# Layer 2's down product in seven block products, with a planned order of instructions

## The chip, the cores and the metric

One core of a Trainium2 chip runs the whole program. The metric is device time in microseconds (us), the median of several runs. The engines that the text speaks of are PE (TensorE, matmuls; PEld is its weight load), ACT (ScalarE), DVE (VectorE), POOL (GpSimd) and SP (SyncE, which issues most of the DMA transfers). Each runs its own instructions in a fixed order and waits on semaphores for the others.

## The reference

A long convolution by FFT, and then two feed-forward layers on the 6016 tokens that come out of it, all in fp32:

```python
X = np.fft.rfft(x, axis=1)                      # x: (2, 3008, 256)
y = np.fft.irfft(X * (filt_r + 1j * filt_i), n=3008, axis=1)
x = y.reshape(6016, 256)
...
h = x @ w_in                                    # layer 1: (256, 2048), (2048, 256)
g = np.where(h >= 1, h, np.where(h <= -1, 0.0, (h + 1) ** 2 / 4))
x = g @ w_out
...
h = x @ w_in2                                   # layer 2, the same sizes
g = h / (1 + np.exp(-h))
return g @ w_out2
```

## The kernel before

**Numbers as sums of two.** Each fp32 factor of a product in the two layers is held as a high part (rounded to the fp32r format by ACT) and a low part (the remainder, a subtraction on DVE, or on POOL for weights). A product is then three matmuls: high by high, high by low, low by high. A matmul here is 128x128 weights by 128x502 (or 128x500) columns.

**The tiling.** The 2048 hidden units are 16 strips of 128, taken as 8 pairs j. The tokens are 12 blocks of about 501, taken as 6 pairs p. The first half of layer 1 (pairs 0 to 2, up to 368.6 us) is worked block by block, while the FFT of the second batch and the preparation of the weights run beside it. From there on comes a list of nine token pairs (`PL`): layer 1's last three, then all six of layer 2. For each of the nine pairs and each j there is one step (`group`), 72 steps in all. A step forms the 2x2 blocks of h (two strips by two token blocks, over two halves of the 256 inputs) by Strassen's scheme in its Winograd form: seven block products (`prod`) in place of eight, 21 matmuls, in three PSUM banks b, c and d. `snap` copies a state of b to SBUF (s1, u2, u4), and DVE adds these to d or c to form the blocks 11, 22 and 21; block 12 is b's last state. Each block then goes through its activation (`Chain.first`, `square`, `last`), is split into high (`high`, ACT, L592) and low (`low`, DVE, L595), and goes down: `down2` multiplies it by the two strips of w_out, 6 matmuls for each of the four blocks, 24 a step, accumulated over j in the banks a0, a1, b0, b1. The down product of step q-1 is issued in the four gaps of step q (`between`). So a step has 45 matmuls on PE.

**What sets the order.** The order in which the code calls the engines is the order of each queue: `group` is written out by hand, and an agenda (`at`, `due`) puts the preparation of operands and weights into numbered slots, four to a step (slot `GA + 4 * q` is the start of step q). Token operands of a pair are seven sums or blocks, split on ACT and DVE during the pair before (`split_x2`, L538; `rest_x2`, L543; `sum_x`, L533). For layer 1, `load_block` forms x by the FFT's last stage, fp32 matmuls (L333). Layer 2's weights are summed, rounded and split once (`sum_weight`, `round_weight`, `rest_weight`: DVE, ACT, POOL) around the start of layer 2, and then lie in SBUF to the end. Outputs are stored from ACT's queue and from SP's (`evict`).

```python
        accumulate(acc[p, n], W[m, j][mate], (chain.gh, chain.gl), first, last)
...
                down2(prev[("11", "22", "12", "21")[i]], (0, 1, 1, 0)[i], (0, 1, 0, 1)[i])
            due(GA + 4 * q + i)
```

## Time and profile before

| | |
|---|---|
| runs | 1140.82, 1142.73 and 1149.37 us, median 1142.73 us |
| span of the profiled execution | 1142.1 us |
| FFT and first half of layer 1 | 0 to 368.6 us |
| second half of layer 1, 24 Strassen steps | 368.6 to 638.0 us |
| layer 2, 48 Strassen steps | 638.0 to 1132.6 us |
| the rest, with the last stores | 1132.6 to 1142.1 us |
| busy share of the span | PE 98%, ACT 73%, DVE 67%, POOL 22% |

The span runs from the first to the last instruction of one execution, and lies 0.6 us under the median of the runs. Matmuls are pipelined, and each row of one is longer (0.39 us) than the distance to the next; how fast PE goes is read from the number of matmuls in a stretch.

### The profile page before, as it was taken

What the parts mean: (1) busy time and instruction counts of PE and PEld (TensorE: products, weight loads), DVE (VectorE), ACT (ScalarE), POOL (GpSimd) and SP (SyncE); (2) the same over time, 40 slices, a digit from 0 to 9 for tenths busy, and PEclk for the clock granted to TensorE, in tenths of its full rate; (3) what the DMA queues carried; (4) which work ended last, traced back from release to release, by engine and by line L of the source; (5) the groups of instructions that cost most, each with busy time, mean ns of one, the idle gap of its engine ahead of it and who ended that gap; (6) DMA issues with size and microseconds to landing.
All of it is one profiled execution on the core that took longest, in us unless ns stands there. A gap on an engine that the chain in (4) does not pass through costs nothing.

```text
span 1142.1 us, 14102 instructions
## 1 busy us (share of the span) xinstructions
PE 1116.0 (98%) x4931; PEld 902.2 (79%) x4931; DVE 764.4 (67%) x1212; ACT 830.2 (73%) x1532; POOL 250.4 (22%) x220
## 2 busy tenths in 40 slices
PE   9899999999999999999999999999999999999998
PEld 3477787787887787888887778888888888888887
DVE  7977656878769788767777766555555555455543
ACT  6788777878767688878888876766666666666654
POOL 5777535657523111000012141000000000000000
PEclk9899999999999999999999999999999999999999
DMA  9433032444221000100211220200200200200100
GB/s 206 130 102 100 3 118 83 136 118 135 92 96 61 28 1 1 37 1 1 81 38 28 76 71 1 72 1 1 73 1 1 73 1 1 73 1 1 37 1 36
DMA packets 34231, 60.33 MB, mean 53 GB/s; under 512 B 3792, under 2 KB 18352, under 8 KB 34160
## 3 DMA queue, kind: packets, MB, share of 16 engines
q1 hardware_dynamic: 30448, 53.03, 15.6%
q10 hardware_dynamic: 3712, 6.40, 1.6%
q8 instruction: 38, 0.62, 0.3%
q14 instruction: 33, 0.27, 0.1%
HBM read 42.90 MB, written 16.52 MB: 52 GB/s over the span
## 4 chain that ended last, share of the span: by engine, by line
PE 76%; DVE 10%; ACT 6%; issue 4%; POOL 2%; DMA 2%; SPq 0%; ACTq 0%; DVEq 0%; POOLq 0%
PE o L395 13%; PE o L394 13%; PE o L396 13%; PE b L547 5%; PE b L549 5%; PE b L548 5%; PE c L547 3%; PE xp L333 3%; PE c L549 3%; PE c L548 3%; PE h L361 2%; DVE we L179 2%; PE h L363 2%; PE h L362 2%; DVE gl L382 2%
## 5 line engine op out<-in xcount | busy, mean ns | idle before, releaser
L394 PE MATMUL o<-gh,wh 128*128 128x502 f32 (+1 forms) x624 | 244.5, 392 | 1.0 <-DVE ob L406 0.7
L395 PE MATMUL o<-gl,wh 128*128 128x502 f32 (+1 forms) x624 | 244.2, 391 | 0.9 <-DVE gl L595 0.6
L396 PE MATMUL o<-gh,wl 128*128 128x502 f32 (+1 forms) x624 | 243.6, 390 | 0.0
L595 DVE TENSOR_TENSOR gl<-c,gh 128x502 fp32r<-128x502 f32 (+1 forms) x288 | 191.2, 691 | 39.9 <-ACT gh L592 39.7
L592 ACT ACTIVATE gh<-c 128x502 fp32r<-128x502 f32 (+1 forms) x288 | 168.1, 617 | 5.7 <-DVE c L584 2.8
L556 ACT ACTIVATE u<-b 128x502 f32<-128x502 f32 (+1 forms) x144 | 83.9, 583 | 106.0 <-PE b L549 105.8
L394 PEld LDWEIGHTS o<-gh,wh 128*128 128x128 f32 x624 | 117.6, 188 | 27.0 <-DVE ob L406 1.5
L395 PEld LDWEIGHTS o<-gl,wh 128*128 128x128 f32 x624 | 117.7, 189 | 26.8 <-DVE gl L595 2.8
L396 PEld LDWEIGHTS o<-gh,wl 128*128 128x128 f32 x624 | 117.6, 188 | 24.5
L669 DVE TENSOR_TENSOR c<-c,u 128x502 f32<-128x502 f32 (+1 forms) x72 | 48.9, 679 | 97.9 <-ACT u L556 97.9
L571 ACT ACTIVATE c<-c 128x502 f32<-128x502 f32 (+1 forms) x144 | 88.7, 616 | 26.9 <-DVE c L669 25.4
L380 ACT ACTIVATE gh<-g 128x502 fp32r<-128x502 f32 (+1 forms) x96 | 59.8, 623 | 54.6 <-PE o L396 30.5
L382 DVE TENSOR_TENSOR gl<-g,gh 128x502 fp32r<-128x502 f32 (+1 forms) x80 | 64.3, 804 | 47.3 <-ACT gh L380 47.2
L688 DVE TENSOR_TENSOR c<-c,u 128x502 f32<-128x502 f32 (+1 forms) x72 | 48.9, 679 | 64.1 <-PE c L549 63.9
L556 ACT ACTIVATE s<-b 128x502 f32<-128x502 f32 (+1 forms) x72 | 42.5, 590 | 61.1 <-PE b L549 59.9
L361 PE MATMUL h<-xh,wh 128*128 128x502 f32 (+1 forms) x192 | 76.8, 400 | 3.6 <-DVE g L374 3.6
L374 DVE SCALAR_TENSOR_TENSOR g<-u,h 128x502 f32<-128x502 f32 (+1 forms) x96 | 64.3, 670 | 23.3 <-ACT u L373 23.3
L363 PE MATMUL h<-xh,wl 128*128 128x502 f32 (+1 forms) x192 | 75.1, 391 | 1.3 <-POOL wl L198 1.3
L362 PE MATMUL h<-xl,wh 128*128 128x502 f32 (+1 forms) x192 | 74.7, 389 | 0.0
L632 DVE TENSOR_TENSOR c<-d,s 128x502 f32<-128x502 f32 (+1 forms) x72 | 48.8, 678 | 37.0 <-ACT s L556 33.4
L367 ACT ACTIVATE u<-h 128x502 f32<-128x502 f32 (+1 forms) x96 | 55.4, 577 | 13.9 <-PE h L363 13.4
L584 DVE SCALAR_TENSOR_TENSOR c<-v,c 128x502 f32<-128x502 f32 (+1 forms) x72 | 49.2, 689 | 22.4 <-ACT v L579 22.1
(199 smaller groups left out, 2414.0 us busy)
## 6 DMA issues: line engine op xcount, KB each, us to landing
f<-in_filt_dram SPq DMA_DIRECT2D x47, 192.0 KB, 3.4
raw<-in_moe_w_in_dram SPq DMA_DIRECT2D x32, 256.0 KB, 2.7
raw<-in_moe_w_out_dram SPq DMA_DIRECT2D x32, 256.0 KB, 3.1
w2d<-wa SPq DMA_DIRECT2D x16, 256.0 KB, 3.4
wb<-w2d SPq DMA_DIRECT2D x16, 256.0 KB, 2.8
xs<-x2d SPq DMA_DIRECT2D x8, 502.0 KB, 4.6
Z<-in_x_dram SPq DMA_DIRECT2D x16, 192.0 KB, 4.9
x<-in_x_dram SPq DMA_DIRECT2D x16, 192.0 KB, 3.6
```

Of the source, the lines that this page charges most:

```text
L361: nc.tensor.matmul(h, wh[:, s], xh[:, k, :t], start=(k == 0), stop=False)
L362: nc.tensor.matmul(h, wh[:, s], xl[:, k, :t], start=False, stop=False)
L363: nc.tensor.matmul(h, wl[:, s], xh[:, k, :t], start=False, stop=(k == 1))
L394: nc.tensor.matmul(o[e], wh[:, s], gh, start=first, stop=False)
L395: nc.tensor.matmul(o[e], wh[:, s], gl, start=False, stop=False)
L396: nc.tensor.matmul(o[e], wl[:, s], gh, start=False, stop=last)
L547: nc.tensor.matmul(bank, wh, xh, start=first, stop=False, skip_group_check=True)
L548: nc.tensor.matmul(bank, wh, xl, start=False, stop=False, skip_group_check=True)
L549: nc.tensor.matmul(bank, wl, xh, start=False, stop=True, skip_group_check=True)
L556: nc.scalar.activation(v, src, AF.Copy)
L592: nc.scalar.activation(self.gh, self.g, AF.Copy)
L595: nc.vector.tensor_tensor(self.gl, self.g, self.gh.bitcast(F32), ALU.subtract)
```

## The change

Nothing changes in what is computed. Up to the end of layer 1's first half two orders change: the down product of a slot stands ahead of the splits of that slot and of the FFT's last stage, and so do its evictions. From the Strassen part on:

- **Down in seven products.** In layer 2 four steps (four j) make a unit group h, 12 of them. The four blocks of each step give four differences or sums on DVE (`combine`: T3, T2, T4, T1), seven operands are split (`halves`), and 7 products by blocks and sums of w_out, for each of 4 j, are 28 units of three matmuls (`UNITS`, `unit`), in place of 96 matmuls. They accumulate in three banks and a fourth (`D`) that takes a copy; `post` adds the results to the outputs, over two unit groups for each token pair. A step has seven gaps, with a unit in each; in layer 2's first four steps there are fewer, and what is left over stands at the end.
- **Snapshots from bank to bank.** The first product of a step is issued in the step before (`start`), ACT copies bank b to bank d, and the second product accumulates upon it, in place of a copy to SBUF and an addition on DVE. The two other snapshots go to SBUF as before.
- **Weights of layer 2.** In steps 11 to 21 the blocks and sums of layer 2's weights are formed, split and stored to memory (`stage2`, `sums2`, `round2`, `rest2`, `store2`). The up weights are then loaded again for each of the 48 steps into a ring of four (`load_up`, 896 KB each); the down weights are loaded once over layer 1's (`load_down`).
- **A planned order.** From `nc.hold()` on, every call is queued, and a planner with a time for each kind of instruction gives them out: PE in the order of the code, each other engine by the earliest start and then by what PE needs first. All stores go through SP. [...]

```diff
-    nc = tc.nc
+    nc = Planner(tc.nc)
...
+        if engine == "PE":
+            busy = n / 2400 + 0.019 if "32r" in ins[0][5] else n / 600 + (0.067 if n < 128 else 0)
+            return busy, busy + 0.19, False
+        if engine == "ACT":
+            busy = n / 1400 + (0.11 if psum else 0.152)
+            return busy, busy + 0.15, False
+        if engine == "DVE":
+            busy = n / 960 + 0.065
+            return busy, busy + 0.14, len(ins) - psum >= 2
+        busy = n / 425 + 0.06
+        return busy, busy + 0.17, True
...
+                for op in q[:1] if e == "PE" else q:
+                    if op.left:
+                        continue
+                    ready = max([o.done for o in op.need if e != "PE" or o.engine != e], default=0.0)
+                    start = max(ready, free)
+                    if op.port:
+                        start = max(start, self.ports["POOL" if e == "DVE" else "DVE"])
+                    key = (start, op.due, op.at)
...
+    def rest2(j, i):
+        h, q = (flat2(j, hl, i // 2)[:, i % 2 * 448:(i % 2 + 1) * 448] for hl in (1, 0))
+        nc.gpsimd.tensor_tensor(q.bitcast(F32R), q, h, ALU.subtract)
...
+    def load_up(g):
+        nc.sync.dma_start(upr[g % 4].bitcast(F32), w2u[g % NP])
...
+    DOWN = {1: ("A11", "a", "B"), 2: ("A12", "c", "D"), 6: ("S2", "a", "B"), 7: ("S3", "b", "C"),
+            5: ("S1", "a", "B"), 3: ("S4", "d", "B"), 4: ("A22", "c", "C")}
...
+        def start(self):
+            self.prod(self.b, "A11", "B11", True)
+            nc.scalar.activation(self.d, self.b, AF.Copy)
...
+        def halves(self, name):
+            h, l = rot("gh")[:, :self.n], rot("gl")[:, :self.n]
+            nc.scalar.activation(h, self.v(name), AF.Copy)
+            nc.vector.tensor_tensor(l, self.v(name), h.bitcast(F32), ALU.subtract)
+            return h, l
+
+        def combine(self):
+
+            for name, to, x0, x1, op_, need in (
+                ("T3", "b", "d", "b", ALU.subtract, {"T3"}), ("T2", "a", "a", "b", ALU.add, {"T3", 1}),
+                ("T4", "c", "c", "a", ALU.subtract, {"T2", 2}), ("T1", "a", "d", "a", ALU.subtract, {"T4", 6}),
+            ):
...
+        k.prod(k.d, "A12", "B21", False)
+        gap(0)
+        k.act("a", k.d)
+        k.prod(k.b, "S2", "T2", False)
+        k.snap("c")
+        gap(1)
...
+    EXTRA = {1: (2, 3), 2: (2, 3), 3: (2, 6)}
+    AHEAD, LOOK = 3, 1
```

The three places on which the prediction rests most, as the built programs have them.

The start of the Strassen part, PE before: bank b0, bank d0, then the leftover down product of layer 1's first half (o, from gh and gl).

```order
L396 MATMUL o5_1_3460<-gh5_10_3647,wl0_10_995 128x500
L547 MATMUL b0_0_3774<-xr_3349,wh0_0_483 128x502
L548 MATMUL b0_0_3774<-xr_3349,wh0_0_483 128x502
L549 MATMUL b0_0_3774<-xr_3349,wl0_0_484 128x502
L547 MATMUL d0_0_3780<-xr_3349,wh0_0_483 128x502
L548 MATMUL d0_0_3780<-xr_3349,wh0_0_483 128x502
L549 MATMUL d0_0_3780<-xr_3349,wl0_0_484 128x502
L394 MATMUL o5_0_3459<-gh5_11_3675,wh0_11_1053 128x500
```

PE now: h_2 is the bank d, h_0 the bank b, and o_b0 the bank of the down product.

```order
L152 MATMUL o_b1_94<-gh_3_83,wl0_11_1051 128x500
L156 MATMUL h_2_3600<-wh0_0_518 128x512
L156 MATMUL h_0_3598<-xr_3200,wh0_0_518 128x502 x2
L156 MATMUL h_0_3598<-xr_3200,wl0_0_519 128x502
L156 MATMUL h_2_3600<-xr_3200,wh0_0_518 128x502 x2
L156 MATMUL h_2_3600<-xr_3200,wl0_0_519 128x502
L156 MATMUL o_b0_93<-gh_0_80,wh0_12_1105 128x500
```

ACT at that place, before and then now; gh is the rounding of the last block of the first half.

```order
L380 ACTIVATE gh5_14_3757<-g5_14_3729 128x500
L373 ACTIVATE u5_15_3755<-u5_15_3755 128x500
L380 ACTIVATE gh5_15_3770<-g5_15_3754 128x500
L556 ACTIVATE s10_0_3778<-b0_0_3774 128x502
L556 ACTIVATE u20_0_3809<-b0_0_3774 128x502
```

```order
L152 ACTIVATE gh_2_82<-g5_14_3553 128x500
L152 ACTIVATE u5_15_3577<-u5_15_3577 128x500
L152 ACTIVATE gh_3_83<-g5_15_3576 128x500
L156 ACTIVATE h_2_3600<-h_0_3598 128x502
L156 ACTIVATE wh0_5_720<-sl_wa2_3614 128x128
```

One row of the leftover down product has gone ahead, and bank d, which waits for ACT's copy of b, now stands ahead of the others; the copy has the place of the snapshot s1, behind the rounding of the last block.

DVE in the middle of layer 2, before: one step and the next one's first rows.

```order
L632 TENSOR_TENSOR c115_3_8064<-d5_3_8060,s15_3_8058 128x500
L595 TENSOR_TENSOR gl21_5_2_8068<-c215_2_8038,gh21_5_2_8067 128x500
L595 TENSOR_TENSOR gl11_5_3_8083<-c115_3_8064,gh11_5_3_8082 128x500
L543 TENSOR_TENSOR xr_3349<-xs6_0_7884,xr_3349 128x502
L669 TENSOR_TENSOR c225_3_8104<-c5_3_8095,u45_3_8102 128x500
L688 TENSOR_TENSOR c215_3_8122<-c5_3_8095,u25_3_8086 128x500
L595 TENSOR_TENSOR gl22_5_3_8125<-c225_3_8104,gh22_5_3_8124 128x500
L595 TENSOR_TENSOR gl12_5_3_8128<-c125_3_8117,gh12_5_3_8127 128x500
L543 TENSOR_TENSOR xr_3349<-xs6_1_7886,xr_3349 128x502
L632 TENSOR_TENSOR c115_4_8149<-d5_4_8145,s15_4_8143 128x500
```

DVE now, some two thirds of a step: sl_ and ob are buffers of blocks, h_3 the bank c.

```order
L156 TENSOR_TENSOR sl_raw_3611<-sl_raw_3611,sl_g10_5833 128x500
L156 TENSOR_TENSOR gl_0_84<-sl_raw_3611,gh_0_80 128x500
L156 TENSOR_TENSOR xr_3200<-xs_1_3226,xr_3200 128x502
L156 TENSOR_TENSOR gl_1_85<-sl_g1_5824,gh_1_81 128x500
L156 TENSOR_TENSOR sl_wa0_3612<-h_3_3601,sl_wa0_3612 128x500
L156 TENSOR_TENSOR gl_2_86<-sl_g6_5829,gh_2_82 128x500
L156 TENSOR_TENSOR sl_raw_3611<-sl_raw_3611,sl_g6_5829 128x500
L156 TENSOR_TENSOR xr0_3616<-xs_1_3226,xr0_3616 128x502
L156 TENSOR_TENSOR gl_3_87<-sl_g0_5823,gh_3_83 128x500
L156 TENSOR_TENSOR sl_g1_3607<-sl_wa0_3612,sl_g1_3607 128x500
L156 TENSOR_TENSOR sl_g2_5825<-h_3_3601,sl_g2_5825 128x500
```

Seven remainders (gl) a step in place of four, two additions from a bank in place of three, and the differences between SBUF blocks are new.

DVE at the end of the program, before and then now.

```order
L595 TENSOR_TENSOR gl11_8_7_10463<-c118_7_10445,gh11_8_7_10462 128x500
L669 TENSOR_TENSOR c228_7_10483<-c8_7_10474,u48_7_10481 128x500
L688 TENSOR_TENSOR c218_7_10500<-c8_7_10474,u28_7_10466 128x500
L595 TENSOR_TENSOR gl22_8_7_10503<-c228_7_10483,gh22_8_7_10502 128x500
L595 TENSOR_TENSOR gl12_8_7_10506<-c128_7_10495,gh12_8_7_10505 128x500
L595 TENSOR_TENSOR gl21_8_7_10518<-c218_7_10500,gh21_8_7_10517 128x500
L406 COPY ob1_11p_1_10542<-o2_8_1_1_9981 128x500
L406 COPY ob1_10p_1_10554<-o2_8_0_1_9964 128x500
```

```order
L156 TENSOR_TENSOR gl_2_86<-sl_raw_3611,gh_2_82 128x500
L156 TENSOR_TENSOR gl_3_87<-sl_g3_5826,gh_3_83 128x500
L156 TENSOR_TENSOR sl_raw21_5839<-o_b0_93,sl_raw21_5839 128x500
L156 TENSOR_TENSOR gl_0_84<-sl_we_3610,gh_0_80 128x500
L156 TENSOR_TENSOR gl_1_85<-sl_wa0_3612,gh_1_81 128x500
L156 TENSOR_TENSOR gl_2_86<-sl_g1_3607,gh_2_82 128x500
L156 TENSOR_TENSOR gl_3_87<-ob_1_89,gh_3_83 128x500
L156 TENSOR_TENSOR sl_wl1_5841<-o_b1_94,sl_wl1_5841 128x500
L156 TENSOR_TENSOR sl_raw21_5839<-o_a1_92,sl_raw21_5839 128x500
L156 TENSOR_TENSOR sl_wh1_5840<-o_b0_93,sl_wh1_5840 128x500
```

Where the last step's two additions, four remainders and two copies stood, a run of splits, differences and additions into the outputs (sl_raw, sl_wl, sl_wh from banks o) now ends the program; of DVE, 37 instructions come after the last up product, of PE 69 matmuls.

## Rows read from the trace of the kernel before

**Rows 1.** The page, part 1: busy us, share, instructions

```profile
PE 1116.0 (98%) x4931; PEld 902.2 (79%) x4931; DVE 764.4 (67%) x1212; ACT 830.2 (73%) x1532; POOL 250.4 (22%) x220
```

**Rows 2.** Stretches of the Strassen part, with clock and DMA

```profile
core 0: us, PE busy (x) PEld busy (x) DVE busy (x) ACT busy (x) POOL busy (x), PEclk, DMA share, GB/s
...
368.57:384.61 16.04, 12.07 (x52) 9.46 (x51) 13.09 (x23) 10.96 (x23) 3.10 (x3) 1.00 0.05 17
384.61:400.61 16.00, 16.00 (x98) 14.22 (x97) 10.73 (x21) 10.35 (x20) 1.69 (x2) 1.00 0.09 33
400.61:637.97 237.36, 234.14 (x1041) 191.05 (x1040) 185.20 (x315) 199.35 (x374) 19.00 (x17) 1.00 0.07 23
...
648.22:661.36 13.14, 11.05 (x47) 8.25 (x45) 8.50 (x13) 9.74 (x19) 6.71 (x6) 1.00 0.67 208
661.36:1122.39 461.03, 461.03 (x2027) 381.72 (x2025) 248.55 (x393) 302.91 (x549) 11.04 (x9) 1.00 0.07 23
```

**Rows 3.** Waits of PE, PEld, 368 to 662 us: total, times, longest

```profile
PE c L547 <- DVE c L669: 3.6, 5, 1.7
...
PEld c L547 <- DVE c L669: 6.6, 7, 2.1
```

**Rows 4.** Timeline, PE, the last matmul of the kernel

```profile
1137.81 0.38 PE L396 MATMUL o<-gh,wl 128*128 128x500 f32 x1
```

**Rows 5.** Timeline of the first step: start, us, instruction, idle before

```profile
371.78 0.49 PE L547 MATMUL d<-xr,wh 128*128 128x502 f32 x1 [2.36 <-DVE g L374]
...
375.09 0.67 DVE L374 SCALAR_TENSOR_TENSOR g<-u,h 128x500 f32<-128x500 f32 x1
...
375.85 0.62 ACT L380 ACTIVATE gh<-g 128x500 fp32r<-128x500 f32 x1 [0.88 <-DVE g L374]
376.38 0.57 ACT L556 ACTIVATE s<-b 128x502 f32<-128x502 f32 x1
...
377.05 0.47 PE L547 MATMUL b<-xr,sh 128*128 128x502 f32 x1 [1.61 <-issue]
```

**Rows 6.** Timeline of ACT in layer 2, a PSUM source and then SBUF sources

```profile
803.35 0.59 ACT L571 ACTIVATE c<-b 128x502 f32<-128x502 f32 x1
803.84 1.13 ACT L592 ACTIVATE gh<-c 128x502 fp32r<-128x502 f32 x2
```

**Rows 7.** Timeline of DVE, 427 to 432 us

```profile
427.33 0.67 DVE L533 TENSOR_TENSOR xs<-xs 128x502 f32<-128x502 f32 x1
427.92 1.27 DVE L584 SCALAR_TENSOR_TENSOR c<-v,c 128x502 f32<-128x502 f32 x2
429.11 0.68 DVE L533 TENSOR_TENSOR t<-xs,xs 128x502 f32<-128x502 f32 x1
429.70 0.68 DVE L669 TENSOR_TENSOR c<-c,u 128x502 f32<-128x502 f32 x1
430.29 2.09 DVE L595 TENSOR_TENSOR gl<-c,gh 128x502 fp32r<-128x502 f32 x2
```

**Rows 8.** Groups of POOL, 400 to 700 us: busy us, mean ns, idle before

```profile
L452 POOL TENSOR_TENSOR wl<-wb,wh 128x512 fp32r<-128x512 f32 x10 | 13.2, 1340 | 46.3 <-ACT wh L449 46.3
L452 POOL TENSOR_TENSOR sl<-ws,sh 128x384 fp32r<-128x384 f32 x8 | 9.7, 1218 | 23.0 <-ACT sh L449 23.0
```

**Rows 9.** DMA issues: KB each, median us to landing

```profile
xs<-x2d SPq DMA_DIRECT2D x8, 502.0 KB, 4.6
...
wb<-w2d SPq DMA_DIRECT2D x16, 256.0 KB, 2.8
```

**Rows 10.** The remainders of the down operands on DVE, layer 2

```profile
L595 DVE TENSOR_TENSOR gl<-c,gh 128x502 fp32r<-128x502 f32 (+1 forms) x180 | 120.0, 687 | 37.0 <-ACT gh L592 37.0
```

**Rows 11.** Timeline of POOL beside rows 7

```profile
430.34 1.50 POOL L452 TENSOR_TENSOR s<-ws,s 128x384 fp32r<-128x384 f32 x1 [9.00 <-ACT s L449]
```

**Rows 12.** A stretch in which the granted clock fell

```profile
40.00:45.80 5.80, 3.88 (x11) 1.65 (x10) 5.76 (x10) 4.18 (x7) 4.72 (x5) 1.00 0.00 2
45.80:52.60 6.80, 5.95 (x18) 3.74 (x17) 5.32 (x10) 3.32 (x6) 5.08 (x5) 0.50 0.24 80
```

More of the change, by code (lines that the diff above doesn't have):

```diff
@@ L494, in up_weight, with up_part, down_part @@
+    def up_part(g, which):
+        a = ORDER.index(which) * 128
+        return [upr[g % 4][:, i, a:a + 128] for i in range(2)]
+    def down_part(j, which):
+        t, c = divmod(7 * j + ORDER.index(which), 4)
+        return [dw[t, i][:, c * 128:(c + 1) * 128] for i in range(2)]
     def up_weight(m, j, which):
@@ new lines, in second_slots, with third_slots @@
+    def second_slots():
+        free[:] = [t for t in free if t.tensor.name not in retired]
+        for t in fixed["wa"]:
+            spare(t)
+    def third_slots():
+        for i in range(13):
+            spare(gp.tile([128, PMAX], F32, name=f"sl_g{i}"))
+        for i in range(2):
+            spare(rings["ob"][i])
+            spare(rawp.tile([128, 1024], F32, tag="raw2", name=f"sl_raw2{i}", bufs=2), 2)
+            for v in "hl":
+                spare(pools["w"].tile([128, 512], F32, tag=f"w{v}", name=f"sl_w{v}{i}"))
+        for name in ("11", "21", "22", "12"):
+            fixed[name] = free.pop()
@@ new lines, in mark_written, with post @@
+    def mark_written(bank):
+        w = weights[0, 0][0]
+        nc.tensor.matmul(bank, w[:, :128], w, start=True, stop=True, skip_group_check=True)
+    def post(h, r, n):
+        i, jj = UNITS[r]
+        if jj != CH - 1:
+            return
+        pair, half = divmod(h, 2)
+        name = {1: "11", 2: "11", 6: "21", 5: "22", 7: "22", 3: "12", 4: "21"}[i]
+        v, src = fixed[name][:, :n], down_bank(h, DOWN[i][2])[:, :n]
+        if i == 1:
+            nc.scalar.activation(down_bank(h, "D")[:, :n], src, AF.Copy)
+        elif i in (2, 6, 5, 3) and half == 0:
+            nc.scalar.activation(v, src, AF.Copy)
+        else:
+            nc.vector.tensor_tensor(v, src, v, ALU.add)
+        if half == 1 and i in (2, 7, 3, 4):
+            e, k = int(name[0]) - 1, int(name[1]) - 1
+            t0 = BLOCKS[2 * pair + k][0]
+            nc.sync.dma_start(out[e * 128:(e + 1) * 128, t0:t0 + n], v)
@@ new lines, in unit, with step, gap @@
+    def unit():
+        u = count["unit"]
+        count["unit"] += 1
+        pump(u)
+        h, r, i, q = unit_of(u)
+        a, _, to = DOWN[i]
+        n = groups[q].n
+        first = UNITS[r] in ((1, 0), (7, 0))
+        triple(down_bank(h, to)[:, :n], down_part(groups[q].j, a), parts.pop(u), first)
+        post(h, r, n)
+        pump(u + AHEAD)
+    def step(q, done=range(7)):
+        k = groups[q]
+        prev = groups.get(q - 1)
+        halves = [("a", 0), ("a", 1), ("d", 0), ("d", 1), ("b", 0), ("b", 1), ("c", 0), ("c", 1)]
+        def gap(i):
+            if i % 2 == 0:
+                spare_bank[0] = k.other
+                due(GA + 4 * q + i // 2)
+            if q <= Q2:
+                if prev:
+                    for name, e in halves[i:i + 1 if i < 6 else i + 2]:
+                        prev.down(name, e)
+                else:
+                    for fn in left.get(i, ()):
+                        fn()
+            elif q >= Q2 + CH or i in EXTRA[q - Q2]:
+                unit()
+        if prev:
+            prev.act("c")
+            prev.cut_up("c")
+        k.prod(k.d, "A12", "B21", False)
[4 more added lines that the diff above has]
+        gap(1)
+        k.cut_up("a")
+        k.prod(k.c, "S3", "T3", True)
+        gap(2)
+        k.prod(k.b, "S1", "T1", False)
+        k.snap("d")
+        k.join("d")
+        gap(3)
+        if q + 1 < STEPS:
+            groups[q + 1] = Group(q + 1)
+            groups[q + 1].start()
+        k.act("d")
+        k.cut_up("d")
+        gap(4)
+        k.prod(k.b, "S4", "B22", False)
+        k.act("b", k.b)
+        if k.m:
+            k.combine()
+        gap(5)
+        k.cut_up("b")
+        k.prod(k.c, "A22", "T4", False)
+        k.join("c")
+        gap(6)
+        if k.m and q + 4 < STEPS:
+            load_up(q + 4)
+        marks[q + 1] = nc.mark()
@@ L864, in tile_fft_conv_moe_moe @@
             rest = up(c, f)
+            if i >= LAG:
+                down(*slots[i - LAG])
             if len(gq) > 1:
```

577 lines of the change are left out of this document (355 added, 222 removed).

## Prediction

> **What bounds the kernel now.** I read the shares of busy time first, then the Strassen part by stages, then the waits inside the stages. PE is busy for 98% of the span, DVE for 67% and ACT for 73% [rows 1]. In layer 2 this is no average over gaps: between 661.36 and 1122.39 us PE is busy for all of 461.03 us, at full clock, with 2025 weight loads, one for each matmul [rows 2]. That is 0.2277 us for a matmul and 10.25 us for a step of 45. DVE is busy for 54% of this stretch and ACT for 66%. So layer 2 gets faster with fewer matmuls, until DVE or ACT is full.
>
> In the second half of layer 1 there is a little besides matmuls. The first step has 51 matmuls (its 21 and the 30 of five leftover down products), 11.6 us, and takes 16.04 [rows 2]: 4.4 us of waiting. The second takes 16.00, 5.75 over 10.25, which are the FFT's last stage for the next pair (PE is busy throughout). Steps 2 to 23 take 237.36; less 22 x 10.25 and once more 5.75, 6.1 us of waiting, mostly for DVE's additions that free bank c [rows 3]. The second step of layer 2 takes 13.14, 2.9 too many [rows 2]. After the last matmul at 1137.81 + 0.23 [rows 4] the span runs on for 4.1 us, with the last copy and store. In all some 13 us of the Strassen part are waits; the rest is the number of matmuls.
>
> **The change, part by part.**
>
> *Matmuls.* Each of 12 unit groups has 28 x 3 = 84 in place of 4 x 24 = 96, so 144 fewer, and two markers more: 142 x 0.2277 = 32.3 us less of PE. This is certain in number, since the built orders show it.
>
> *The first step.* In the trace ACT rounds the last block of the first half at 375.85, because DVE forms it only at 375.09, and takes the snapshot behind it at 376.38; PE goes on at 377.05 [rows 5]. DVE's backlog there belongs to the part that isn't planned, and its order is kept. The copy from bank to bank has the snapshot's place in ACT's order, but now bank d waits for it, and the leftover down products stand behind d. So by 377.05 PE has done 10 matmuls since 368.57 (six that were moved ahead, a marker, three for b) where it did 18 before. From 377.05 on, 3118 matmuls are left (3122 of the Strassen part less four): 709.9 us. With two last stages of 5.75, PE alone ends at 1098.5, and with the 4.1 us behind it the span is 1102.6. To that come waits.
>
> The copy itself, PSUM to PSUM on ACT, stands nowhere in the trace. It lies between 0.49 and 0.62 us, the shortest distance and the longest duration of ACT's rows [rows 5, 6]; I take the nearest, the snapshot's 0.57. In later steps six matmuls (S4 and A22) lie between the product that it reads and the one that needs it, 1.37 us, which hide it with its waits. It saves one addition a step on DVE, 0.59 us where DVE isn't waited for, so nothing by itself.
>
> *The rest of layer 1.* Costs of an instruction are distances of starts: DVE runs five from 427.33 to 430.29, 0.592 us each [rows 7]; ACT has 0.49 from PSUM and 0.51 from SBUF (two in 1.13, less the 0.62 of one) [rows 5, 6]. ACT's 15 instructions a step stay, 7.6 us. In steps 11 to 21 come 32 roundings of layer 2's weights (448 columns, 0.46 each by length), so with the operands of the next pair ACT has 9.6 to 10.4 us in a step of 10.25: about 95% full. POOL gets 32 remainders of about 1.28 us, between its groups of 384 and 512 columns [rows 8], for 24 before, and all in those steps. DVE has about 8 us a step. The reordering by need should save most of the 6.1 us in the other steps, a full ACT costs some in these; I take 5 us, with 1 and 18 as ends (18: the third rival). The first half's two swaps hold ACT behind six matmuls, 1.4 us, in five slots; a down product comes five slots after its up product, which hides that, and if not it is 7 us. I take nothing.
>
> *Start of layer 2.* Its first four steps hold 24 down matmuls of the last layer-1 step and then only two units each. Three steps of 27 matmuls last 6.1 us. The longest loop through bank c (product S3, a unit, S1, snapshot 0.6, addition 0.68, A22, addition 0.68, with short waits) is some 5.2 us, so PE stays the longer one. I take 2 us, ends 0 and 6. The up weights come from memory now: 896 KB a step. A load of 502 KB lands in 4.6 us [rows 9], so 896 KB in at most 8.2; it is issued three steps ahead, 28 us. On SP the loads stand in one queue with the stores of outputs, which wait for DVE's additions; those are a few us, and the 28 us cover them.
>
> *Steady layer 2.* From the fifth step to the last up product, 44 steps, the built order has 662 instructions on DVE, 15.05 a step: 7 remainders, 4 combinations, 2 additions, and shares of operands and outputs. That is 8.91 us against 42 x 0.2277 = 9.56 on PE: 93%. Steps with 17 have 10.06 us, half a microsecond over PE, and the next step gives it back. Four buffers of splits let ACT and DVE be three units ahead, 3 x 1.37 us with the up products between, where a split needs about 2.2 us (ACT 0.6, DVE 0.68, waits between them). ACT has some 15.2 a step, 7.8 us. So PE should stay the bound; I take 3 us for the whole stretch, ends 0 and 64 (the first rival).
>
> *The end.* Behind the last up product stand 69 matmuls, 15.7 us, and 37 instructions of DVE, 21.9 us. Here DVE is the bound: 6 us more, ends 4 and 10.
>
> The sum: 1102.6 + 5 + 2 + 3 + 6 = 1118.6 of span, and 0.6 for the median over this execution: **1119 us**, 2.1% less than 1142.7.
>
> **Rivals.** Nothing but noise is within about 1% (1131.3 to 1154.2); that is what a measurement of this kernel can tell from no change.
>
> 1. *Slower: DVE waits for each rounding.* Place: steady layer 2, where a remainder follows its rounding on ACT. Before, 180 remainders waited 37.0 us, 0.206 each, and a waiting instruction lasts its full 0.687 [rows 10]. If all seven of a step do so: 7 x 0.893 + 8.05 x 0.592 = 11.0 us a step, 1.46 over PE, 64 us: 1180. It costs the whole gain from 0.18 us of wait in each remainder on. For it: the wait is in the trace and DVE has only 0.65 us a step to spare. Against: there, nothing else stood between, and now four operands are rounded ahead and other work fills in. 0.06.
>
> 2. *Each DVE instruction takes its whole duration*, 0.687 us instead of 0.592: 15.05 x 0.687 = 10.34, 0.78 over PE, 34 us, less the 3 counted, and 3.5 more at the end: 1154. Against it are the five starts 0.592 apart [rows 7]. 0.04. [...]
>
> 3. *ACT and POOL are too full in steps 11 to 21.* Two remainders on DVE beside a POOL subtraction took 2.09 us [rows 7, 11], where 0.592 + 0.687 would be 1.28, so 0.8 more. 32 of these are 26 us of DVE in ten steps, 2.6 a step, where about 2.2 are free; with ACT at 95% I put half of it, 13 us, on PE, above the 5: 1132. For it: the work is dense; against it: it is due late and can give way. 0.14. [...]
>
> 4. *Transfers are late.* From step 11 to 24 some 34 MB are moved (stores and loads of layer 2's weights), in 14 steps or 143 us; at the 208 GB/s that the trace shows at most [rows 2] that is 163 us, 20 more: 1139. Against it: at 208 the share is 0.67. 0.06.
>
> That the change doesn't do what it says is excluded by the built orders. A fall of the clock is in the range: PE pauses for about 6 us in the first step, with four matmuls in it, and after a sparse stretch the clock stood at 0.50 for 6.8 us [rows 12], which would cost 3.4 us here.
>
> **How the numbers follow.** Forecast 0.65, on its own 1109 to 1129; better than that (no waits in layer 1 and layer 2, a shorter end) 0.05, about 1107; the rivals as given. Faster by over 1%: 0.65 + 0.05 + half of rival 3 = 0.77, and 0.01 of rival 4. Slower by over 1%: rival 1 and half of rival 2, 0.08. The same: 0.14. The range 1106 to 1138 leaves out rivals 1 and 2, half of rival 4 and a little below: some 0.16.
>
> **What the profile after would show.** Steps of layer 2 of 9.6 us, with PE busy throughout and DVE near 93%: right. Steps of over 10 us with PE waiting for remainders: rival 1 or 2, told apart by the distance of DVE's starts. The first step: PE waiting at bank d until ACT's copy, about 377. Waits in steps 11 to 21 beside POOL's remainders: rival 3; PE waiting for loads at 600 to 640 us: rival 4. At the end some 22 us with DVE full. What would make it wrong most is a wait in each unit that the counts can't show, since 0.1 us of it in each of 336 is 34 us.

## The result and the profile after

The changed kernel takes 1115.8 us (median of 4 runs, 1112.97 to 1117.07), the kernel before 1143.1 (median of 4, 1140.82 to 1149.37): a ratio of 0.974, with a 95% interval of 0.970 to 0.978. So it is faster by 2.6%, 27 us; 1119 was forecast, with a range of 1106 to 1138. The profiled execution took 1117.07 us and has a span of 1115.3.

The page, part 1, of the changed kernel, to be set beside [rows 1]:

```profile
PE 1088.2 (98%) x4789; PEld 880.4 (79%) x4789; DVE 941.2 (84%) x1512; ACT 913.8 (82%) x1708; POOL 262.7 (24%) x228
```

PE has 142 matmuls fewer and is still busy 98% of the span; DVE has 300 instructions more and went from 67% to 84%. The shares alone say that PE is the bound as before. The stages say where it isn't. The stretches of the Strassen part in the changed kernel, cut at the starts of its d products (the columns are those of [rows 2]):

```profile
core 0: us, PE busy (x) PEld busy (x) DVE busy (x) ACT busy (x) POOL busy (x), PEclk, DMA share, GB/s
...
366.00:373.10 7.10, 1.46 (x6) 0.56 (x4) 6.04 (x9) 4.25 (x8) 0.74 (x1) 0.82 0.10 37
373.10:377.30 4.20, 4.16 (x10) 3.39 (x11) 2.55 (x9) 1.82 (x4) 1.50 (x2) 0.50 0.01 2
377.30:413.30 36.00, 34.60 (x178) 29.29 (x178) 25.06 (x47) 26.44 (x52) 5.15 (x7) 1.00 0.04 15
413.30:637.15 223.85, 221.82 (x994) 182.94 (x993) 181.40 (x292) 196.98 (x377) 46.38 (x36) 1.00 0.42 147
637.15:670.75 33.60, 31.46 (x129) 24.64 (x128) 22.14 (x37) 24.23 (x45) 0.00 (x0) 0.95 0.45 154
670.75:1080.97 410.22, 410.22 (x1808) 340.26 (x1807) 388.98 (x649) 357.56 (x669) 0.00 (x0) 1.00 0.34 115
1080.97:1115.30 34.33, 27.21 (x106) 20.09 (x104) 29.62 (x50) 19.45 (x34) 0.00 (x0) 0.94 0.08 30
```

The row from 670.75 on is steady layer 2: 43 steps of 9.54 us in which PE is busy for all of the time and DVE for 95%. Before it stand two places where PE waits (366 to 377, 637 to 671), behind it one (1081 on); in all three the clock's mean is under 1.

The first of them, in the timeline of the first Strassen step (to be set beside [rows 5]; the first row is the marker, a product by `mark_written` into bank d; behind it h on PE and ACT is first bank b, then bank d, "h<-h" the copy from one to the other):

```profile
366.11 0.40 PE L156 MATMUL h<-wh 128*128 128x512 f32 x1
...
367.92 0.72 PE L156 MATMUL h<-xr,wh 128*128 128x502 f32 x2 [1.41 <-DVE g L152]
...
371.99 0.62 ACT L152 ACTIVATE gh<-g 128x500 fp32r<-128x500 f32 x1 [0.88 <-DVE g L152]
372.52 0.57 ACT L156 ACTIVATE h<-h 128x502 f32<-128x502 f32 x1
...
373.14 1.21 PE L156 MATMUL h<-xr,wh 128*128 128x502 f32 x2 [4.27 <-ACT h L156]
```

PE does four matmuls between 366.11 and 373.14, and waits for the copy, which stands on ACT behind the rounding of the first half's last block. The copy itself lasts 0.57 us. The granted clock falls to 0.50 inside this wait (a mean of 0.82 from 366.00 to 373.10 puts the fall near 370.5), and PE's first 10 matmuls behind the wait, until 377.3, still run at it (the second row of the stretches).

The second place, at the start of layer 2 (ob<-o_a is the copy with which DVE empties a bank of layer 1's sums):

```profile
651.00 0.59 ACT L156 ACTIVATE sl_wa<-h 128x502 f32<-128x502 f32 x1 [1.03 <-PE h L156]
651.62 0.68 DVE L156 TENSOR_TENSOR sl_wa<-h,sl_wa 128x502 f32<-128x502 f32 x1 [1.41 <-ACT sl_wa L156]
652.22 0.67 DVE L156 COPY ob<-o_a 128x500 f32<-128x500 f32 x1
...
652.94 0.49 PE L156 MATMUL o_a<-gh,wh 128*128 128x502 f32 x1 [1.98 <-DVE ob L156]
```

DVE's copy stands behind an addition that waits 1.41 us for ACT, and PE waits 1.98 us for the bank.

### The profile page after: what moved, and what is told of

The parts are those of the page before. It is cut to its first block, busy times and chain, and to the rows that moved or that the text cites. A ratio compares the mean times of both kernels' runs of the same rounds, so it can differ in the third digit from the quotient of the medians.

```text
span 1115.3 us, 14796 instructions
## 1 busy us (share of the span) xinstructions
PE 1088.2 (98%) x4789; PEld 880.4 (79%) x4789; DVE 941.2 (84%) x1512; ACT 913.8 (82%) x1708; POOL 262.7 (24%) x228
## 4 chain that ended last, share of the span: by engine, by line
PE 71%; DVE 13%; ACT 8%; issue 4%; POOL 2%; DMA 2%; SPq 0%; ACTq 0%; DVEq 0%; POOLq 0%
PE h L156 28%; PE o_a L156 15%; PE o_b L156 13%; PE h L152 6%; PE o_a L152 5%; DVE gl L156 2%; DVE we L152 2%; PE xp L152 2%; PE o_b L152 1%; DVE gl L152 1%; PE s L152 1%; ACT gh L152 1%; DVE g L152 1%; ACT u L152 1%; POOL hl L152 1%
## 5 line engine op out<-in xcount | busy, mean ns | idle before, releaser
L156 PE MATMUL h<-xr,ur 128*128 128x502 f32 (+1 forms) x1008 | 283.2, 391 | 0.2
L156 PEld LDWEIGHTS h<-xr,ur 128*128 128x128 f32 x1008 | 190.7, 190 | 40.9 <-ACT sl_g L156 0.6
L156 DVE TENSOR_TENSOR gl<-sl_g,gh 128x502 fp32r<-128x502 f32 (+1 forms) x205 | 140.2, 688 | 16.6 <-ACT gh L156 16.1
L156 ACT ACTIVATE gh<-sl_g 128x502 fp32r<-128x502 f32 (+1 forms) x205 | 126.6, 620 | 27.3 <-PE o_a L156 10.6
L156 PE MATMUL o_a<-gh,wh 128*128 128x502 f32 (+1 forms) x288 | 113.5, 394 | 3.9 <-DVE ob L156 2.0
L156 PE MATMUL o_a<-gl,wh 128*128 128x502 f32 (+1 forms) x288 | 113.5, 394 | 2.3 <-DVE gl L156 2.2
L156 PE MATMUL o_a<-gh,wl 128*128 128x502 f32 (+1 forms) x288 | 112.7, 391 | 0.0
L156 PE MATMUL o_b<-gl,wh 128*128 128x502 f32 (+1 forms) x248 | 97.2, 392 | 0.4 <-DVE gl L156 0.4
L156 PE MATMUL o_b<-gh,wh 128*128 128x502 f32 (+1 forms) x248 | 97.5, 393 | 0.0
L156 PE MATMUL o_b<-gh,wl 128*128 128x502 f32 (+1 forms) x248 | 97.0, 391 | 0.0
```

The costliest lines, as they stand in the source:

```text
L156: op = Op(engine, lambda: call(*args, **kwargs), busy, until, port)
```

## The experiments

Times by stage, in us, are read from the trace of each kernel's profiled execution, between starts of PE's products: the third up product to the last (the first half of layer 1, where no instruction is planned), from there to the fourth d product (the first three Strassen steps), to step 24 (the rest of layer 1), to step 28 (the start of layer 2), to step 71 (steady layer 2), to the last matmul (the end). A stage that a kernel leaves alone agrees with the changed kernel's within some 0.4 us (the first half within 1), or within 0.7 in the first steps and 1.3 at the start of layer 2, where the clock fell to 0.50 in the changed kernel's execution; so a few us can be told here that the medians alone wouldn't tell.

```
kernel           median    first half  3 steps  layer 1   start   steady     end
changed          1115.8      299.97     51.28   223.84    33.59   410.22   30.09
old slot order   1119.4      305.04     51.13   224.18    33.61   410.54   29.67
code order       1321.4      299.11     60.37   348.78    39.76   470.91   32.42
no due times     1124.1      299.94     50.85   229.44    31.13   416.99   29.61
8 products       1146.9      299.13     51.92   223.78    36.28   437.55   31.61
1 DVE more       1123.8      299.28     51.87   223.78    32.31   416.58   32.03
2 DVE more       1148.0      300.08     51.54   223.84    33.63   437.93   33.77
via SBUF         1123.9      300.05     49.85   227.38    32.25   414.59   29.75
first step       1109.9      300.10     46.16   223.80    32.02   410.24   30.32
+ banks          1106.6      300.11     46.18   223.83    29.82   410.24   30.18
+ POOL           1113.3      300.05     46.19   223.77    29.82   410.24   37.86
```

### Is the gain the matmuls? Eight products' worth of them

```
         v = parts.pop(u)
         triple(down_bank(h, to)[:, :n], down_part(groups[q].j, a), v, first)
+        if i == 1:
+            triple(down_bank(h, to)[:, :n], down_part(groups[q].j, a), v, False)
```

> In layer 2 each unit of the first down product is multiplied twice, so that a group has 32 units' worth of matmuls instead of 28; DVE, ACT and all else are the same (the first product is counted twice, so the output is another). It has 144 matmuls more, as many as the eighth block product had. Theory (PE is the bound throughout layer 2 and what the change gave there is the number of matmuls): 144 x 0.2277 = 32.8 us more, steps of 10.22 us in place of 9.54, the whole 1148 to 1149. Rival (DVE's work sets the steps and PE only follows it, so that PE has room): less than 20 us more, the whole under 1136.

1146.9 us (median of 10), ratio to before 1.0035 (1.0017 to 1.0052): 31.1 more than the changed kernel. In the steady stretch 120 of the 144 matmuls cost 27.33 us, 0.2278 each; at the start of layer 2 another 12 cost 2.7; at the end the last 12, which are 2.7 us of PE, cost 1.5, since PE waits there anyway. The theory holds, and the rival falls. With the old number of matmuls the rest of the change together (planned orders, differences on DVE, copies between banks, the first half's order) is worth nothing: the kernel is 4 us slower than before, though the first half alone gains 5 us (a later experiment).

### How full is DVE? One and two remainders more

```
         v = self.halves(DOWN[i][1])
+        if i in (1,):                      # the second kernel: (1, 6)
+            nc.vector.tensor_tensor(v[1], self.v(DOWN[i][1]), v[0].bitcast(F32), ALU.subtract)
```

> In layer 2 the remainder of the first down product's operand is formed twice in a row on DVE, which is one instruction more a step, 16.05 in place of 15.05. Theory (a DVE instruction takes 0.592 us, so DVE has 9.50 us a step against PE's 9.56 and is just not the bound): steps 9.54 to 9.65 us, 0 to 5 us more over the 44 steps and some 2 us more at the end, the whole 1116 to 1123. Rival (the order has no room, each remainder's wait for ACT eats what is left of DVE's step, so each instruction more lengthens the step by its whole 0.6 to 0.69 us): steps 10.15, 26 to 30 us more, the whole 1142 to 1148.

> As the run with one, but the remainders of two of the seven down products' operands are formed twice, 17.05 instructions on DVE a step. Theory (0.592 us each): DVE has 10.09 us a step, 0.53 over PE, so steps of 10.1 us, 44 x 0.55 = 24 us more and some 4 us more at the end: 1140 to 1147. Rival (PE is the bound with room to spare and DVE's idle time takes it in): steps of 9.55 us, under 1122. Third case (a cost of 0.687 us each): 17.05 x 0.687 = 11.7 us a step, 1210.

One more: 1123.8 us, 8 over the changed kernel. Two more: 1148.0, 32 over it, ratio to before 1.0045 (1.0027 to 1.0064), which is the whole gain. Both are a little over the upper end of the theory (1123 and 1147) and far from its rivals. The price is as supposed; the steady stretch of the kernel with two more:

```profile
669.39:1107.32 437.93, 419.89 (x1808) 338.00 (x1806) 434.30 (x734) 361.09 (x669) 0.00 (x0) 1.00 0.31 108
```

DVE is busy for 99% of it, and 434.30 over 734 instructions is 0.592 us each; at 0.687 they would take 504. What the theory missed is over which steps the mean was taken. DVE's work repeats with each token pair, that is every eight steps. The 15.05 is the mean over all 44 steps, with lighter ones at both ends of the stretch; in a full eight DVE starts 122 to 124 instructions, 15.4 a step. Eight steps of the changed kernel and of that with one remainder more (the counts of DVE take in one or two that only overlap an end):

```profile
718.43:794.95 76.52, 76.52 (x338) 63.41 (x336) 73.63 (x125) 66.68 (x125) 0.00 (x0) 1.00 0.36 124
```

```profile
720.02:797.95 77.93, 76.90 (x338) 63.24 (x337) 77.88 (x132) 66.83 (x125) 0.00 (x0) 1.00 0.36 121
```

With one more there are 131 in eight steps, and 131 x 0.592 = 77.6 us is more than the 76.2 to 76.5 that PE takes: DVE is the bound and has no idle time left (77.88 of 77.93 us). With two more, 139 x 0.592 = 82.3, and eight steps take 82.0 to 82.2. PE waits out the difference in few of the steps: with one more, 38 of 43 keep their 9.5 us and every eighth, five in all, has 10.7 to 11.0. In the timeline of DVE and PE in one of these five:

```profile
724.43 0.68 DVE L156 TENSOR_TENSOR ob<-ob,sl_wl 128x502 f32<-128x502 f32 x1
725.02 0.68 DVE L156 TENSOR_TENSOR ob<-sl_raw,ob 128x502 f32<-128x502 f32 x1
725.61 0.68 DVE L156 TENSOR_TENSOR gl<-sl_g,gh 128x502 fp32r<-128x502 f32 x1
...
726.34 0.49 PE L156 MATMUL o_b<-gl,wh 128*128 128x502 f32 x1 [1.03 <-DVE gl L156]
```

DVE runs back to back, 0.59 us from start to start, and PE waits 1.03 us for the remainder that was third in the row. In the changed kernel DVE is idle for 2.9 of 76.5 us in eight steps, which is less than one instruction a step.

### Does the order matter? Code order, and no due times

```
-    nc.hold()                                          # code order
     mark_written(rings["h"][2])
...
-                    key = (start, op.due, op.at)       # no due times
+                    key = (start, op.at, op.due)
```

> The list scheduler is never switched on: every engine has its instructions in the order in which the code is written, and seven of layer 1's first outputs leave by ACT's queue; the products, the differences on DVE and the copies from bank to bank stay. Theory A (the planned orders are what lets DVE run at 0.592 us an instruction and 93% of its time; in code order each remainder stands right behind its rounding on the other engine and waits about 0.2 us, and the evictions stand in the wrong place): steps of layer 2 of 10.5 to 11.2 us in place of 9.54, the whole 1160 to 1200, slower than before. Theory B (PE is the bound and the buffers of splits cover the order): steps of 9.6 us, the whole within 10 us of 1116.

> The changed kernel with the list scheduler's tie-break by need taken out: among instructions that could start at the same moment, the one first written goes first, not the one whose user on PE is due first. Theory (what the scheduler gives over the written order is mostly that nothing stands behind an instruction that can't start; the due times decide only among those that are ready, and DVE at 93% and ACT at 95% in steps 11 to 21 need them there): layer 2's steps 9.55 to 9.75 us, layer 1's a few us of waits more in steps 11 to 21, the whole 1118 to 1130. Rival A (due times don't matter): 1116. Rival B (they are what the scheduler gives): steps of 10.5 us or more in layer 2, 1150 and over.

In code order: 1321.4 us, ratio 1.155 (1.152 to 1.158). Theory A had steps of layer 2 of 10.5 to 11.2, and they are 10.95 on average; it gave layer 1 nothing, and there the steps are 16.6 us, 125 us more in all. So its 1160 to 1200 is far too low, though it was right on the side and on layer 2. Its waits of DVE in steady layer 2, then those of the changed kernel in its own steady stretch (columns as in [rows 3]):

```profile
DVE gl L152 <- ACT gh L152: 45.8, 71, 1.3
DVE gl L152 <- PE h L152: 6.3, 5, 1.3
```

```profile
DVE gl L156 <- ACT gh L156: 20.1, 34, 1.0
```

A remainder still waits for its rounding in the planned order, but half as often and with nothing else beside it. A layer-1 stretch of the kernel in code order:

```profile
435.00:517.00 82.00, 65.39 (x228) 50.40 (x227) 43.88 (x75) 48.33 (x87) 4.56 (x6) 0.83 0.00 1
```

No engine is full: ACT and DVE are busy for 59% and 54%, PE idles for 17 us and its clock's mean is 0.83. They wait for each other in turn (in this stretch DVE 15.4 us for roundings on ACT, ACT 16.9 us to round what DVE forms). This code isn't the order that was written by hand before, so the 206 us are what the new code needs of the scheduler, not what scheduling would give to the old one.

Without due times (the ranking by what PE needs first) it is 1124.1 us, 8 more than with them. In steady layer 2 steps are 9.70 on average: every eighth again has 10.7, and waits of a remainder for its rounding make 27.5 us where they were 20.1. In the rest of layer 1 it is 5.6 us more. The theory holds: looking past instructions that can't start gives nearly all, the ranking by need the last 8 us.

### What is the copy from bank to bank worth?

```
         def start(self):
             self.prod(self.b, "A11", "B11", True)
-            nc.scalar.activation(self.d, self.b, AF.Copy)
+            nc.scalar.activation(self.take("a"), self.b, AF.Copy)
...
-        k.prod(k.d, "A12", "B21", False)
+        k.prod(k.d, "A12", "B21", True)
         gap(0)
-        k.act("a", k.d)
+        nc.vector.tensor_tensor(k.v("a"), k.d, k.v("a"), ALU.add)
+        k.act("a")
```

> The copy from bank b to bank d is undone alone: ACT takes the first product to an SBUF block again, the product of d starts a fresh sum, and DVE adds the two; that is one instruction of DVE more a step (16.05 in layer 2, and one more in layer 1), and the marker in bank d goes. Theory (bank to bank is worth only DVE time that PE doesn't wait for): layer 2's steps 9.55 to 9.65, layer 1's 10.24 with some 2 to 5 us more of waits in steps 11 to 21, the first step 2 to 4 us shorter since PE doesn't wait for the copy: the whole 1112 to 1122. Rival (DVE is the bound when it has one instruction more on the path from d to the activation): steps over 10 us, the whole over 1140.

1123.9 us, 8 more, against 1112 to 1122 expected; the stages add up to 5: 4.4 in steady layer 2, 3.5 in the rest of layer 1, 1.4 less in the first steps and 1.3 less at the start of layer 2. Every eighth step of layer 2 takes 10.2 to 10.6 us, as with one remainder more, and DVE starts 130 to 132 instructions in eight steps. So the copy is worth one DVE instruction a step, and that counts where DVE is full; a "nothing by itself" it is not. The 3 us between the two sums are no more than runs of one kernel differ by. The rival of steps over 10 us throughout falls.

### The first half's order of a slot, undone

```
             rest = up(c, f)
-            if i >= LAG:
-                down(*slots[i - LAG])
             if len(gq) > 1:
                 split_g()
             act_rest(*rest)
             if f == (15 if c == 0 else 8) and c not in (1, NS - 1):
...
                 prep_x(nx, 1)
+            if i >= LAG:
+                down(*slots[i - LAG])
```

> The first half of layer 1 goes back to the old order of a slot: split, activation, then where it stands the FFT's last stage for the next block, and the down product behind all of them; everything from the second half of layer 1 on is as in the changed kernel. Theory (the down product and the evictions ahead of the last stage are worth about 1.6 us at each of the places (2,8) and (3,8) and less at (4,8)): the start of up product (4,10) is 3.5 to 5 us later than in the changed kernel, the steps before (2,8) are equal within 0.3 us, and the whole is 1119 to 1121. Rival (the 4 us came from another cause, such as the clock's falls in the FFT part, and the swap is worth nothing, as the prediction had it): the starts agree within 1 us and the whole is 1116.

1119.4 us, 3.6 more; the first half takes 305.04 us where ten kernels with the new order have 299.1 to 300.1. Besides what is shown, this run takes the buffers of gh and gl one by one from the pool, as the kernel before did, four of each as in the ring. With (block, strip) for an up product, the steps stand where the last stage of the FFT is done for the next block: 1.6 us at (2,8), 2.3 between (3,6) and (3,9), 0.8 in block 4. The theory holds, and the mechanism is in the timeline of the old order at (2,8) (xp is the last stage):

```profile
169.16 2.76 PE L152 MATMUL xp<-dft_sb,Z 128*128 128x92 f32 x24
...
171.75 0.47 PE L152 MATMUL o_a<-gh,wh 128*128 128x502 f32 x1
...
173.42 0.62 ACT L152 ACTIVATE gh<-g 128x502 fp32r<-128x502 f32 x1 [3.06 <-PE o_a L152]
...
175.41 0.50 PE L152 MATMUL h<-xh,wh 128*128 128x502 f32 x1 [1.33 <-DVE g L152]
```

The rounding gh needs the buffer that the down product frees; the down product stands behind 24 matmuls of the last stage, so ACT waits 3.06 us, the activations behind it come late, and PE waits 1.33 us for a bank. With the down product ahead, ACT's wait there is 0.72 us and PE has none.

### The two waits that were left, mended

```
-    split_g()
...
+    rest[0]()
     mark_written(rings["h"][2])
     groups[0] = Group(0)
     groups[0].start()
+    split_g()
+    rest[1]()
+    rest[2]()
+    first_slots()
+    nc.hold()
...
-            banks[h, name] = out_bank[("a0", "a1", "b0")[len(banks) % 3]]     # second kernel
+            banks[h, name] = out_bank[("a0", "b0", "a1")[len(banks) % 3]]
```

> In the first Strassen step the leftover down products whose operands are ready stand ahead: one ahead of the marker and of the first product of b, two between that product and the product of d, and the copy from bank b to bank d stands ahead of the rounding of the first half's last block on ACT. Theory (PE's waits of 1.41 and 4.27 us there, and the half clock from 370.5 to 377.3, come from PE having nothing ready ahead of bank d): PE has 22 matmuls done by 371.3 where it had 4 by 373.14, the granted clock stays at 1.00 through the step, the second step starts 6 to 9 us earlier, and the whole is 1107 to 1110. Rival (DVE's backlog is the bound of the first two steps and PE would only wait later, at the last leftover product or at bank b): the second step starts less than 3 us earlier, the whole is 1113 to 1116.

> The mended first step as in the run before, and the sums of down products in layer 2 take the banks in the order a0, b0, a1 in place of a0, a1, b0, so that the second unit isn't put in the bank whose last layer-1 sum DVE copies out behind an addition. Theory (PE's wait of 1.98 us for that copy at the second step of layer 2 is the bank's): that step is 2 us shorter and the rest is unchanged, the whole 1107.5 to 1108.5. Rival (another wait takes its place, on bank h or on the addition itself): less than 0.7 us shorter, the whole 1109 to 1110.

With the first step filled: 1109.9 us, ratio to before 0.970 (0.966 to 0.973), 5.9 under the changed kernel. The second step starts 5.1 us earlier, short of the 6 to 9 of the theory; the whole is in its range, because the start of layer 2 is 1.6 shorter too: in this execution the clock is 1.00 there (640 to 670 us), where it was at 0.50 for 3.2 us in the changed kernel's. That isn't shown to be the edit's doing, since with one remainder more that start is 1.3 shorter too (32.31), and that kernel has the changed kernel's first step. The first step's timeline:

```profile
366.96 0.49 PE L152 MATMUL o_b<-gl,wh 128*128 128x500 f32 x1 [0.81 <-DVE gl L152]
...
368.43 0.62 PE L152 MATMUL h<-xr,wh 128*128 128x502 f32 x2
...
372.23 0.61 PE L156 MATMUL h<-xr,wh 128*128 128x502 f32 x2
```

The d product starts at 372.23, with 22 matmuls behind it where there were four, and PE waits only 0.81 us, for DVE; the clock is 1.00 from 358 to 390 us. The rival (DVE's backlog comes next) has its share: from 374 to 382 us PE is busy for only 5.7 us of 8.

With the banks changed as well: 1106.6 us, ratio 0.968 (0.965 to 0.970), median of 5, a little under the 1107.5 to 1108.5 of the theory. The start of layer 2 is 2.2 us shorter than with the first step alone, as expected, so the wait was the bank's. The stretches of this kernel, first steps and start of layer 2:

```profile
365.00:369.70 4.70, 4.55 (x20) 3.49 (x19) 3.72 (x6) 4.25 (x8) 0.00 (x0) 1.00 0.09 33
...
629.15:658.98 29.83, 29.45 (x129) 23.59 (x127) 21.36 (x36) 23.59 (x45) 0.00 (x0) 1.00 0.51 173
```

PE is busy for 29.45 of 29.83 us where it was for 31.46 of 33.60. This is the fastest of all, 9 us under the changed kernel.

### The end: differences on POOL

```
-                    nc.vector.tensor_tensor(self.v(to), self.v(x0), self.v(x1), op_)
+                    (nc.gpsimd if self.q >= STEPS - 3 else nc.vector).tensor_tensor(
+                        self.v(to), self.v(x0), self.v(x1), op_)
```

> As the run with the first step and the banks mended; besides, the 12 differences of the last three layer-2 steps are formed on POOL, which is idle there, and not on DVE. Theory A (POOL's subtraction takes about 1.3 us and a remainder on DVE beside it takes some 0.8 us more, as in layer 1's 2.09 us for two): DVE is relieved of 12 x 0.592 = 7.1 us and pays 12 x 0.8 = 9.6 us, and the operands of the differences come later; the stretch from the last d product to the last matmul, 30.2 us now, gets 0 to 4 us longer, the whole 1106 to 1111. Theory B (the two engines don't hold each other up): the stretch is 4 to 5 us shorter, since its excess over 105 matmuls, 6.3 us, is DVE's, and the whole is 1102.

1113.3 us, 6.7 more than without it and over theory A's 1106 to 1111; the end takes 37.86 us for 30.18, so theory A is right on the sign and had the size at half. Its timeline, POOL and then DVE:

```profile
1079.87 1.68 POOL L156 TENSOR_TENSOR sl_wa<-sl_wa,sl_g 128x500 f32<-128x500 f32 x1
1082.16 1.64 POOL L156 TENSOR_TENSOR sl_g<-sl_g,sl_u 128x500 f32<-128x500 f32 x1 [0.61 <-DVE gl L156]
```

```profile
1078.70 1.75 DVE L156 TENSOR_TENSOR sl_we<-sl_we,sl_g 128x500 f32<-128x500 f32 x1
1080.37 3.97 DVE L156 TENSOR_TENSOR gl<-sl_g,gh 128x500 fp32r<-128x500 f32 x3
1084.28 0.68 DVE L156 TENSOR_TENSOR gl<-ob,gh 128x500 fp32r<-128x500 f32 x1
```

Three remainders beside POOL's two differences take 3.97 us where they take 1.9 alone, and the instruction ahead of them 1.75 for 0.67. POOL's own go from 1.27 to some 1.6. Theory B falls. But not all of the 7.7 us is DVE's. The end of this kernel, and then of the one without POOL:

```profile
1069.00:1107.00 38.00, 30.99 (x106) 21.64 (x104) 29.97 (x38) 19.17 (x34) 15.49 (x11) 0.82 0.05 17
```

```profile
1069.20:1099.60 30.40, 26.99 (x106) 20.13 (x104) 28.74 (x49) 19.43 (x34) 0.00 (x0) 0.94 0.02 9
```

PE is busy for 4.0 us longer with the same matmuls: 22 of them run at the lower clock, for 7 without POOL. The rest, some 3.6 us, is idle time, and PE's waits for remainders on DVE go from 2.2 to 5.8 us. How much of that is DVE held up and how much operands that come later from the slower engine was not told apart.

## Why the prediction held, point by point

*The sum.* It went from the d product's start to the end of PE's work without waits, 721.45 us, and added 16 us of waits. Measured from that start (373.14) to the end of the last matmul (1111.06 + 0.23) are 738.15: 16.7 us of waits. That this is so near 16 is in part luck: 3 us too many in steady layer 2 stand against 2.7 too few at its start and 1.6 too few in layer 1. The mechanism holds: PE is the bound, and the gain is the number of matmuls. The terms one by one:

- Matmuls: 0.2277 us each was right to 0.0001 in the run with 144 more.
- First step: PE waits at bank d for the copy, as said; the start came at 373.14, not 377.05, wholly because of the first half (next point). The copy was put at 0.57 us and lasts 0.57. The fall of the clock that was kept in the range for 3.4 us came: 10 matmuls at half clock, 2 us, besides 1.7 us of waits in the next two steps. Filling the first step gave 5.1 us of the waits there back.
- The first half's swaps, costed at nothing: they gave 5.1 us (305.04 against 299.97). This step failed. The prediction looked for what the swap could cost ACT and didn't ask what frees the buffers that ACT writes: the down product does. Between the profiled executions of before and after 3.9 us of it are seen, since in that of after the first half began some 1.3 us later.
- The rest of layer 1: 5 forecast, 6.6 measured (3.7 in the first three steps, with the clock's 2, and 2.9 in the rest).
- The copy from bank to bank, put at "nothing by itself": it saves some 5 us by the stages, most of it in steady layer 2. This was undersized: with one DVE instruction more a step a full eight steps are some 131 x 0.592 = 77.6 us of DVE, over PE's 76.3, though the mean over the whole stretch (16.05 x 0.592 = 9.50) is under PE's 9.56.
- The start of layer 2: 2 forecast, 4.7 measured, inside its ends of 0 and 6. The loop through bank c that was reckoned there wasn't it. A bank emptied late was, 2.2 us, and behind it the clock stood at 0.50 from 653.9 to 657.1 us, some 1.6 us more.
- Steady layer 2: 3 forecast, none found; 43 steps are 1.0 us under 43 x 9.56. The two pairs of 500 columns have some 9.53 us a step, but one of 502 has as little, so why is open. DVE's 93% by count (15.05 x 0.592) are 95% in a full eight steps (123 x 0.592 = 72.8 of 76.3 us), so there was less to spare than the 0.65 us a step that the prediction set against its first rival.
- The end: 6 forecast, 6.4 measured. DVE runs back to back from 1089 to 1097 there and PE waits for it, but a fall of the clock to 0.50 from 1101.0 to 1104.4 is in it too, with 7 matmuls, at most some 1.3 us that the sum didn't have.

With 3.9 gained ahead and 0.7 more waits the span is 1115.3 for 1118.6.

*Rival 1, DVE waits for each rounding.* It had 11.0 us a step, and the kernel in code order has 10.95. That the two agree is luck: the mechanism is real, but there 71 of some 300 remainders wait, not all, and other waits share the steps; in the planned order 34 of some 300 remainders wait, 20.1 us in all, and DVE's spare time takes that in. The argument against it, other work between a rounding and its remainder, is what the planned order provides and the code order doesn't.

*Rival 2, each instruction takes its whole duration.* It is out: 0.592 us each in 734 instructions with DVE 99% busy. At its whole 0.687 each that stretch would be 504 us (an estimate, 734 x 0.687); it took 437.93.

*Rival 3, ACT and POOL too full in steps 11 to 21.* POOL's 32 remainders are there, 1.35 us each for the 1.28 forecast (the group of them, to be set beside [rows 8]):

```profile
L156 POOL TENSOR_TENSOR w2s<-w2s 128x448 fp32r<-128x448 f32 x32 | 42.4, 1346 | 142.1 <-DVE w2s L156 81.8 <-ACT w2s L156 31.7 <-ACT c L156 14.0
```

They cost little: the waits of steps 11 to 23 are 3.5 us in all (1.4 in step 13, 0.3, 0.3, 0.9 and 0.6 in later ones), since DVE is busy for 87% of that stretch and ACT for 92% (95% was forecast for ACT). At the end, where it is full, 12 instructions moved to POOL cost 7.7 us, with the later operands and the lower clock (a mean of 0.82 for 0.94). There a DVE instruction with both inputs in SBUF took up to 1.75 us beside POOL, for 0.67 alone. So the work on POOL cost at most 3.5 us in the stretch where DVE was busy for 87%, and 7.7 where it was busy for 95% (28.74 of 30.40 us with the differences on DVE).

*Rival 4, transfers.* PE waits for none of them. The traffic in one of 40 slices reached 345 GB/s, well over the 208 on which the rival stood, and an up weight of 896 KB lands 4.7 us after its issue in the median, for the at most 8.2 that were reckoned (the DMA issues, to be set beside [rows 9]):

```profile
ur<-w2u SPq DMA_DIRECT2D x48, 896.0 KB, 4.7
```

So the highest rate seen in the trace before was no ceiling.

## What to carry to other kernels

When PE is the bound, the worth of fewer matmuls is their number times their spacing in that stage (0.228 us here), until the next engine is full; count the other engine's instructions by the distance of starts (0.592 us here), and over one full repetition of the work (eight steps here) rather than over a stretch with lighter ends. By the one mean DVE had room for one instruction more a step, by the other it hadn't; that one cost 8 us, and the second another 24. When code is put in another order, ask which buffer each instruction frees and who waits to write it: the down product behind the FFT's last stage held up ACT, and nothing in its own row said so. And look at a new wait together with the clock behind it: with 5.7 us of waiting in the first step the clock was at 0.50 from 370.5 to 377.3 us, and with products that were ready in its place it was 1.00 and the second step started 5.1 us earlier, for a few lines moved.

## What the runs showed of the hardware

- The clock falls at different times in executions with the same instructions up to that point. In the stretch from 46 to 57 us, still the FFT, the granted clock was 0.53 in the changed kernel's execution and 0.52 in that with one remainder more, and 1.00 in those of the old slot order, of the copy through SBUF and of the first step and banks mended. The third up product started anywhere from 58.5 to 65.1 us. So up to 6.6 us between two executions are decided ahead of it, about as much as the runs of one kernel differ by (4 us in the changed kernel, 6 in that with eight products).
- In the first Strassen step the clock fell to 0.50 near 370.5 us, when PE had begun four matmuls since 366.1; with the same stretch filled it was 1.00 from 358 to 390 us.
- ACT copies 502 columns from one PSUM bank to another in 0.57 us, as fast as from PSUM to SBUF (0.57 to 0.59), and matmuls add to what it wrote. In these kernels a marker product has been through the bank before; whether it is needed no run shows.
- In the run with differences on POOL four single DVE instructions of 500 columns with both inputs in SBUF that began while POOL's ran took 1.44 to 1.75 us (1071 to 1089 us), and one 0.84; alone such an instruction takes 0.67.
